# A transformer block on one core with another order of the same operations

## The chip, the cores and the metric

The kernel runs on one core of a Trainium2 chip. A core has five engines that work side by side, each with a queue of its own that it takes strictly in order: TensorE (PE, matmuls), VectorE (DVE), ScalarE (ACT, which evaluates functions), GpSimd (POOL) and SyncE (SP, which here only issues transfers); sixteen DMA engines move the data. Semaphores tie the queues together. Data lie in an on-chip memory of 128 partitions, and PE writes into eight accumulator banks (PSUM), which the other engines read. The metric is the device time of one execution in microseconds, less is better; the median of three executions before is 439.99 us (439.59 to 440.89).

## The reference, cut to what matters

```python
def _A_ref(x, wq, wk, wv, wo, beta):          # x: 1 x 2048 x 576, bf16
    H, Dh, N, L = 32, 18, 4, 512              # 32 heads of 18, 4 segments of 512 tokens
    q, k, v = ...                             # x @ wq, x @ wk, x @ wv, split in heads and segments
    phi = lambda t: jnp.where(t > 0, t + 1.0, jnp.exp(t))
    g = _sigmoid(beta).reshape(1, H, 1, 1)
    M, z = 0, 0
    for s in range(N):
        p = _softmax(qs @ ks^T * Dh ** (-0.5) + causal_mask)
        a_dot = p @ vs
        pq = phi(qs)
        a_mem = (pq @ M) / (pq @ z + 1e-06)
        outs.append(g * a_mem + (1.0 - g) * a_dot)
        pk = phi(ks)
        M = M + pk^T @ vs
        z = z + sum over tokens of pk
    return concat(outs) @ wo

h  = x + _A_ref(_layernorm(x), ...)
h2 = h + gelu(_layernorm(h) @ w1 + b1) @ w2 + b2     # w1: 576 x 4608, w2: 4608 x 576
```

## The kernel before

**Stages.** The 2048 tokens are handled as four segments of four tiles of 128 rows. Per segment s the program has these stages, whose letters stand in the names of its operations: X (first layer normalization: statistics at L814, the centring or scaling at L844 to L848, then a transposition of the result, on PE at L865 for some tiles, by a transfer at L726 for the others), P (the projections to q, k and v, L924, L954 and L971), A (attention: scores at L1151 or L1311, exponential at L1100 or L1102, causal mask at L1163 or L1166 in segment 0 and L1323 or L1325 later, product with the values at L1182 or L1336, read-out of the memory at L1282, then transposition, reciprocal of the row sum and product at L1196 to L1205), M (the update of the memory: product at L1066, sum into `MZacc` at L1076), B (the product with wo, the residual, second layer normalization), C (first feed-forward product, L1466 and L1509, and gelu) and D (second feed-forward product, L1563, and the last sum, L1576). The stages of different segments run beside one another: while ACT is in the exponentials of one segment, PE has projections and feed-forward products of others.

**Some forms that occur below.** One exponential reads four banks in one instruction of 128x2048 (L1100), or two instructions of 128x1024 (L1102) read two banks each. A projection pair is either ten matmuls over all 128 rows (L954), or two halves of matmuls over 64 rows each (L924), between which another engine passes a mark (L930). A copy (`copy`, L733 to L739) moves a bank to memory on ACT or DVE. After segment 0, q and k go through a buffer in DRAM: a copy writes the pad `qk_pad` (L735 or L739), a transfer of SP stores it to `qkd` (L1025), and a transposing transfer brings it back as `qk`.

**What sets the order.** Every operation is added to a graph under a name: the stage's tag and its own, so `M0macc` are the two sums into `MZacc` of segment 0 and `A01mask` the masks of the second unit of segment 0's attention. The table `TIMETABLE` (L27) gives each of them, in the order of their adding, an engine and a rank: the letter is the engine (p PE, a ACT, d DVE, g POOL, s SP; w stands for an exponential or copy that is merged with its partner in one instruction, u for a part of gelu that ACT does straight from the bank), the number the rank. `Graph.add` reads them:

```python
op.start, op.eng = self.timetable[key, n]
```

`Graph.schedule` sorts all operations by rank, hands out banks and buffers in that order (`Buf.pick` takes the one that came free first), and fuses the halves of a projection where nothing of PE stands between them; the program is then emitted in this order, so that the ranks are the order in every engine's queue. There is no other scheduler behind it.

**Names that the change and the prediction touch.** `ones` (L1608, ACT) fills the column of ones beside the values; the ACT memsets (L713) clear the pads `fk_pad` for phi(k); `gate` (L800) is a copy of one element behind which loads are held until the first x has landed; `gates` (L1617 to L1622) compute sigmoid(beta); X00copy and X1apply are copies of the transposed x of tile 0 and the scaling of segment 1's x; P1qkst are the four stores of segment 1's q and k (L1025), P1copy the copies into their pads.

Of the kernel before, what the change touches and what calls it, by code (L numbers as in the profile page):

```python
# [27 lines left out]
    "A00exp": "a84 w85 a114 a131",  # L28
    "A00mask": "g140 g93 d94 g89 g204 d170 g197 g201",
    "A00st0": "p 73 110",  # L30
    "A01comb": "g 208 209 224 225",
    "A01exp": "a148 a155 a162 a165 a174 w186 a168 a169",
    "A01mask": "g153 d156 g164 g163 d193 d190 d189 g207",
    "A01oT": "d 210 250 253 239 242",
    "A01rec": "d 188 206 215 218",
    "A01st0": "p 139 151 173 167",
    "A01swap": "g241 d238",
    "A01val": "p 171 211",
    "A01valT": "d 177 175 212 214",
    "A02comb": "g 360 401",  # L40
    "A02exp": "a198 w199 a281 w283 a226 w227 a232 w247 a290 w291 a306 a312 a326 a328",
    "A02mask": "g 321 268 270 317 244 260 343 351",
    "A02rec": "d 347 365",
    "A02st0": "p 194 256 213 231 286 301 320",
    "A02val": "p 303 322 349 355",
    "A02valT": "d 339 358",
    "A03comb": "g 487 516",
    "A03exp": "a356 a359 a377 a378 a369 a370 a389 a396 a409 w410 a419 w422 a440 w441",
    "A03mask": "d400 g380 d379 g412 g405 g406 g448 g442",
    "A03oT": "d 512 534 510 539 530",  # L50
    "A03rec": "d 431 478",
    "A03st0": "p 354 371 361 388 407 418 423",
    "A03swap": "g 524 529",
    "A03val": "p 413 416 463 472",
    "A03valT": "d 420 476",
    "A1comb": "g685 g711 g739 g754 g809 g819 d866 d874",
    "A1comb2": "d695 g720 g740 g778 g826 g820 d881 d875",
    "A1eg": "a 397 386 482 653 699 748 807 765",
    "A1exp": "a475 w484 a511 w519 a493 a502 a582 w597 a527 w540 a600 a605 a625 w632 a639 w640 a656 w657 a678 a693 a704 w706 a749 a750 "
        "a728 w729 a779 w780 a783 w784 a759 a760 a814 a815 a831 a832 a837 a846 a794 w796",  # L60
    "A1flip": "s 395 374 457 557 572 592 719 659",
    "A1mask": "g494 g532 g586 g587 g591 d609 g541 d613 g681 d675 g680 d663 d665 g736 g735 d715 d744 g751 g772 d752 g764 g793 g785 d801 "
        "g828 g850 g853 g848 d845 d847 g857 g806",
    "A1mem": "p 583 469 683 742 725 795 839 851",
    "A1memT": "d 584 470 696 743 726 808 840 852",
    "A1memfin": "d674 g652 d717 g777 g812 g816 d869 g873",
    "A1oT": "d 769 871 829 899 905",
    "A1pq": "d 499 446 621 727 700 787 825 803",
    "A1rec": "d 644 619 713 745 775 810 868 862",
    "A1rec2": "d 616 684 705 753 786 818 860 872",  # L70
    "A1rg": "g 498 432 620 598 667 781 800 746",
    "A1st": "p 474 503 492 581 523 599 618 638 655 677 703 747 722 766 782 758 811 830 836 791",
    "A1swap": "d877 g904",
    "A1val": "p 588 614 682 737 773 802 855 858",
    "A1valT": "d 589 617 698 738 774 817 856 859",
    "A2comb": "g972 d1014 d1083 g1103 g1174 g1192 d1240 d1222",
    "A2comb2": "d1017 d1055 d1109 g1138 g1175 d1193 g1248 g1226",
    "A2eg": "a 870 854 1015 994 1070 1089 1156 1182",
    "A2exp": "a895 a896 a864 a879 a888 a900 a883 a884 a903 a906 a998 w999 a1020 w1021 a980 w983 a1026 w1027 a1003 w1004 a1091 a1092 "
        "a1048 w1051 a1105 a1115 a1072 w1073 a1114 a1123 a1131 w1132 a1136 a1137 a1179 a1189 a1154 w1155 a1167 w1176",  # L80
    "A2flip": "s 797 844 912 909 1036 933 1053 1066",
    "A2mask": "g918 d962 g880 d916 d955 g913 d930 d952 d1010 g1037 d1034 g1007 g991 d1046 d1012 g1045 g1098 g1088 g1067 d1116 d1140 "
        "d1104 g1145 d1124 g1162 g1196 d1190 g1206 g1200 d1201 g1215 g1213",
    "A2mem": "p 988 1009 1049 1063 1128 1143 1204 1209",
    "A2memT": "d 1006 1032 1059 1081 1129 1144 1205 1210",
    "A2memfin": "g1016 d1042 g1079 g1125 g1172 g1160 d1243 g1223",
    "A2oT": "d 1056 1230 1263 1257 1252",
    "A2pq": "d 940 927 1018 1062 1094 1097 1178 1183",
    "A2rec": "d 1008 1041 1078 1084 1165 1159 1212 1211",
    "A2rec2": "d 971 989 1082 1102 1150 1149 1233 1221",  # L90
    "A2rg": "g 805 911 986 1030 1044 1096 1130 1164",
    "A2st": "p 892 843 887 882 902 993 1019 973 1025 1002 1076 1043 1100 1061 1110 1120 1135 1177 1153 1161",
    "A2swap": "d 1251 1228",
    "A2val": "p 969 966 1038 1086 1122 1147 1207 1216",
    "A2valT": "d 970 968 1080 1087 1127 1148 1208 1217",
    "A3comb": "g1388 g1389 g1473 d1488 d1529 d1527 d1599 d1604",
    "A3comb2": "g1390 d1435 g1496 d1489 d1531 d1572 d1606 d1605",
    "A3eg": "a 1214 1334 1299 1423 1471 1440 1555 1545",
# [1639 lines left out]
```

## Time and profile before

| | |
|---|---|
| median of three executions | 439.99 us (439.59 to 440.89) |
| profiled execution | 440.23 us |
| its span in the trace | 438.5 us |
| PE busy | 430.4 us, 98% of the span |
| ACT, DVE, POOL busy | 298.1, 271.9, 177.4 us |
| granted TensorE clock | 0.999 |
| moved by DMA | 70.09 MB, 160 GB/s |

The span runs from the first to the last instruction of the trace; 1.7 us of the profiled execution's own time lie outside it. The page's view in 40 slices of 11 us each shows the course: the tenths in which each engine is busy.

```profile
PE   8988999999999999999999999999999999999997
PEld 5765677776677676654445766644457775446775
DVE  6898899898888986975785776856535110000110
ACT  6997889998988898767998867688473002565000
POOL 6687757546768416544413468430112020010010
```

PE is full except in the first four slices and the last. DVE and ACT are nearly full until about slice 16, and have much time left from slice 28 on, when only feed-forward products remain. "idle before" in a row of the trace is the time for which the engine stood still ahead of the instruction, and the arrow behind it names what released it. In rows of the timeline the first number is the start, the second the length from the first to the last of the instructions that a row puts together.

### The profile page before, as it was taken

The page shows a single profiled execution, that of the slowest core. Times are in us where ns is not written, and L with a number is a line of the kernel's source. Part 1 is how long each engine was busy: PE and PEld are TensorE (multiplying, and loading weights), DVE is VectorE, ACT ScalarE, POOL GpSimd, SP SyncE. Part 2 cuts the span into 40 slices and gives each one's busy share as a digit, 9 for nine tenths or more (in the row PEclk, how much of TensorE's full clock was granted, in tenths as well). Part 3 has the DMA queues.
Part 4 walks back from the last instruction along what each step waited for, and adds up shares of the span by engine and source line. Part 5 has one row for each costly group of instructions (what it writes and reads, how often), then busy time and mean ns, then how long its engine had stood idle before and what let it go on. Part 6 is the DMA issues. An engine that isn't in the chain of part 4 may idle for free.

```text
span 438.5 us, 12035 instructions
## 1 busy us (share of the span) xinstructions
PE 430.4 (98%) x5053; PEld 275.3 (63%) x5053; DVE 271.9 (62%) x580; ACT 298.1 (68%) x313; POOL 177.4 (40%) x333
## 2 busy tenths in 40 slices
PE   8988999999999999999999999999999999999997
PEld 5765677776677676654445766644457775446775
DVE  6898899898888986975785776856535110000110
ACT  6997889998988898767998867688473002565000
POOL 6687757546768416544413468430112020010010
PEclk9999999999999999999999999999999999999999
DMA  7799699988999866482833574415554431630020
GB/s 230 181 231 225 258 200 258 297 178 241 239 246 327 160 176 184 109 176 83 229 108 76 122 192 147 105 55 176 175 168 126 112 110 55 230 95 1 19 64 28
DMA packets 77126, 70.09 MB, mean 160 GB/s; under 512 B 58000, under 2 KB 64528, under 8 KB 77072
## 3 DMA queue, kind: packets, MB, share of 16 engines
q1 hardware_dynamic: 76928, 69.23, 59.8%
q8 instruction: 39, 0.64, 0.7%
q14 instruction: 15, 0.12, 0.1%
q10 hardware_dynamic: 144, 0.09, 0.1%
HBM read 42.30 MB, written 13.37 MB: 127 GB/s over the span
## 4 chain that ended last, share of the span: by engine, by line
PE 91%; DMA 3%; DVE 2%; SPq 1%; ACT 1%; issue 0%; POOL 0%; ACTq 0%; DVEq 0%
PE bank L1563 33%; PE bank L1466 24%; PE bank L1509 8%; PE bank L924 7%; PE bank L954 7%; PE bank L1311 5%; PE bank L1336 3%; DMA x<-in_A_x_dram 2%; DMA qkd<-qk_pad 2%; PE bank L1151 1%; PE bank L1285 1%; PE bank L1282 1%; SPq L719 1%; PE bank L1182 1%; PE bank L1066 1%; SPq L726 0%
## 5 line engine op out<-in xcount | busy, mean ns | idle before, releaser
L1563 PEld LDWEIGHTS <-hT 128*128 128x128 bf16 x1152 | 110.4, 98 | 33.8 <-issue 6.1
L1466 PE MATMUL bank<-xreg,w1g 64*128 64x512 bf16 x972 | 108.2, 376 | 0.0
L1100 ACT ACTIVATE pt<-bank 128x2048 bf16<-128x2048 f32 x41 | 77.0, 1877 | 19.6 <-PE bank L1311 10.4
L1102 ACT ACTIVATE pt<-bank 128x1024 bf16<-128x1024 f32 x78 | 75.7, 1022 | 17.4 <-PE bank L1311 11.3
L1466 PEld LDWEIGHTS <-w1g 64*128 64x128 bf16 x972 | 46.8, 94 | 55.7 <-issue 2.8
L1563 PE MATMUL bank<-w,hT 128*128 128x288 bf16 x576 | 77.3, 286 | 0.0
L1563 PE MATMUL bank<-w_lo,hT 128*128 128x288 bf16 x576 | 76.9, 286 | 0.0
L1576 DVE TENSOR_TENSOR ot<-bank,hc 128x288 bf16<-128x288 f32 x32 | 14.2, 454 | 89.0 <-PE bank L1563 82.4
L1472 ACT ACTIVATE hT<-bank,b_col 128x512 bf16<-128x512 f32 x36 | 22.4, 688 | 47.8 <-PE bank L1466 47.7
L1325 POOL TENSOR_SCALAR_AFFINE_SELECT pt<-pt 128x512 bf16<-128x512 bf16 x60 | 39.4, 669 | 32.4 <-ACT pt L1100 19.3
L1549 POOL TENSOR_TENSOR hc<-hc,b_bc 128x576 f32<-128x576 f32 x13 | 16.7, 1287 | 80.7 <-DMA hc<-hd 80.7
L1432 ACT ACTIVATE hT<-hT 128x3072 bf16<-128x3072 bf16 (+8 forms) x18 | 39.8, 2260 | 0.1
L1509 PE MATMUL bank<-xreg,w1g 64*128 64x256 bf16 x648 | 38.1, 269 | 0.1
L1509 PEld LDWEIGHTS <-w1g 64*128 64x128 bf16 x648 | 30.6, 94 | 6.4 <-issue 2.9
L954 PE MATMUL bank<-hT,xreg 128*128 128x288 bf16 x252 | 34.5, 287 | 0.0
L1482 ACT ACTIVATE hT<-bank,b_col 128x512 bf16<-128x512 f32 x36 | 22.9, 684 | 11.3 <-PE bank L1466 11.0
L954 PEld LDWEIGHTS <-xreg 128*128 128x128 bf16 x252 | 23.1, 98 | 8.0 <-issue 0.9
L924 PE MATMUL bank<-hT,xreg 64*128 64x288 bf16 x292 | 23.8, 285 | 0.5 <-ACT pt L1102 0.5
L1311 PE MATMUL bank<-qk 32*128 32x512 bf16 (+3 forms) x384 | 23.8, 301 | 0.0
L1297 POOL TENSOR_TENSOR t<-t,r 128x288 f32<-128x288 f32 x13 | 9.3, 717 | 34.7 <-DVE r L1294 34.6
L1291 DVE STREAM_TRANSPOSE t<-bank 128x512 f32<-128x512 f32 x24 | 16.7, 701 | 7.6 <-PE bank L1282 4.4
L1344 DVE STREAM_TRANSPOSE t<-bank 128x512 f32<-128x512 f32 x24 | 16.4, 692 | 6.7 <-PE bank L1336 5.9
(128 smaller groups left out, 580.3 us busy)
## 6 DMA issues: line engine op xcount, KB each, us to landing
w1g<-in_B_w_dram SPq DMA_DIRECT2D x41, 576.0 KB, 4.4
qkd<-qk_pad SPq DMA_DIRECT2D x12, 512.0 KB, 4.6
hd<-h SPq DMA_DIRECT2D x16, 288.0 KB, 3.9
hc<-hd SPq DMA_DIRECT2D x16, 288.0 KB, 3.7
w_lo<-in_B_w_dram SPq DMA_DIRECT2D x3, 864.0 KB, 6.7
w<-in_B_w_dram SPq DMA_DIRECT2D x3, 864.0 KB, 9.2
xb<-in_A_x_dram SPq DMA_DIRECT2D x16, 144.0 KB, 4.2
out_dram<-ot SPq DMA_DIRECT2D x15, 144.0 KB, 3.6
```

The lines of the kernel that those rows point to most:

```text
L924: return nc.tensor.matmul(out=half(hf), lhsT=xTb.t[r, k, ts], rhs=wt[r, hf, k, :], start=start, stop=stop, skip_group_check=True)
L954: nc.tensor.matmul(out=half(hf), lhsT=xTb.t[:, k, ts], rhs=wt[:, hf, k, :], start=(k == 0 and b.form != "first"), stop=(k == n - 1 and b.f ...
L1100: nc.scalar.activation(out=pt.t[:], in_=banks_all[:, st[0].n:st[0].n + 4, :], func=ACT.Exp, scale=scale)
L1102: nc.scalar.activation(out=pt.t[:, 2 * j:2 * j + 2, :], in_=st[j].t[:], func=ACT.Exp, scale=scale)
L1311: nc.tensor.matmul(out=st[i // 2].t[:, i % 2, off:off + n_], lhsT=qk[rows, 1, kt * P:(kt + 1) * P], rhs=qk[rows, 0, kt * P:L], start=True, ...
L1325: nc.gpsimd.affine_select(out=blk, in_=blk, pattern=[[0, 4], [1, P]], compare_op=ALU.is_ge, fill=0.0, base=0, channel_multiplier=-1)
L1432: nc.scalar.activation(out=at, in_=at, func=ACT.Gelu_apprx_tanh)
L1466: nc.tensor.matmul(out=cc[w].t[:], lhsT=w1.t[rows, k, q, :], rhs=x2T[s].t[rows, k, :], start=(k == 0), stop=(k == ND - 1))
L1472: ready_f[f + w] = [add(pf - 12, {"act": 0.68}, lambda e, f=f, w=w, cc=cc: nc.scalar.activation(out=hT[:, :, f + w, :], in_=cc[w].t[:].rea ...
L1482: nc.scalar.activation(out=dst, in_=src, func=ACT.Identity if e == "act" else ACT.Gelu_apprx_tanh, bias=b)
L1509: nc.tensor.matmul(out=cc[w].t[:, q * 2 * P:(q + 1) * 2 * P], lhsT=w1.t[rows, k, q, :], rhs=x2T[s].t[rows, k, ts], start=(k == 0), stop=(k ...
L1563: nc.tensor.matmul(out=c.t[:, 0:c1 - c0], lhsT=hT[:, tl // 2, f, (tl % 2) * P:(tl % 2 + 1) * P], rhs=w2_c[ch][:, f - ch * WCH, c0:c1], sta ...
```

## The change

The program has the same 1904 operations with the same names, before and after. Only the numbers and letters of `TIMETABLE` differ, in nearly all of its 320 lines; `Graph` and all stages are the same text. A few of the lines, those of which the prediction speaks:

```diff
-    "A00exp": "a84 w85 a114 a131",
+    "A00exp": "a 74 78 103 111",
-    "A01mask": "g153 d156 g164 g163 d193 d190 d189 g207",
+    "A01mask": "g163 d156 g158 g162 d188 d198 g207 d194",
-    "A01rec": "d 188 206 215 218",
+    "A01rec": "d 186 202 223 217",
-    "M0macc": "d 203 196",
+    "M0macc": "d 205 203",
-    "P1qkst": "s 282 254 336 332",
+    "P1qkst": "s 290 213 332 307",
-    "X00copy": "a 22 29 31 36",
+    "X00copy": "a25 d33 a31 a35",
-    "X1apply": "d 185 172",
+    "X1apply": "d 214 173",
-    "P1copy": "d233 a237 a338 d166 a192 a228 d314 a323 a297 a259 a292 d382",
+    "P1copy": "d232 a241 a344 d177 a189 a233 d313 a327 a297 a253 a293 d385",
-    "P01copy": "a118 d137 a105 a102 a107 a138",
+    "P01copy": "d123 d137 d93 a87 a98 a138",
-    "C00copy": "d368 w372 d362 w363 d403 w404 d443 w447 d414 w415 d481 d485 d490 w491 d496 w501 d504 w505",
+    "C00copy": "d376 w377 d364 w367 d403 a420 d434 w455 d424 w431 d489 w490 d461 w469 d495 d496 d511 w512",
...
-    "gate": "g 13",
+    "gate": "d 9",
-    "gates": "a95 d96",
+    "gates": "a95 d169",
-    "memset": "d24 g32 g5 d11 a45 a54 a112 a113 g426 g53 g6",
+    "memset": "d8 g7 g36 d65 a26 a94 a58 a109 g427 g14 g328",
-    "ones": "a 417 47",
+    "ones": "a 38 16",
```

As the letters say, the change moves operations between engines as well: over the program 12 merged exponentials become halves, 33 parts of gelu instead of 21 are done straight from the bank, and PE has 16 more matmuls, since two projection pairs that were fused now have other work between their halves.

Three places show what it moves. The first is ACT's queue at the start of the program. Here x_64 holds the first x, xn_142 and xn_143 its centred copies, mean_b their row sums, and xreg is the transposed x that the projections read. Before:

```order
L825 ACTIVATE xn_142,mean_b_108<-x_64 128x288
L825 ACTIVATE xn_143,mean_b_109<-x_64 128x288
L846 ACTIVATE xn_142<-x_64,mean_b_108 128x2x128
L735 COPY xreg<-bank 128x3x128
L846 ACTIVATE xn_143<-x_64,mean_b_109 128x2x128
L735 COPY xreg<-bank 128x2x128
L735 COPY xreg<-bank 128x3x128
L735 COPY xreg<-bank 128x2x128
L713 ACTIVATE fk_pad_138<-fk_pad_138 128x32x7
L1608 ACTIVATE v_aug_116<-ident 128x128
```

Now:

```order
L825 ACTIVATE xn_142,mean_b_108<-x_64 128x288
L1608 ACTIVATE v_aug_116<-ident 128x128
L825 ACTIVATE xn_143,mean_b_109<-x_64 128x288
L846 ACTIVATE xn_142<-x_64,mean_b_108 128x2x128
L735 COPY xreg<-bank 128x3x128
L713 ACTIVATE fk_pad_138<-fk_pad_138 128x32x7
L846 ACTIVATE xn_143<-x_64,mean_b_109 128x2x128
L735 COPY xreg<-bank 128x3x128
L735 COPY xreg<-bank 128x2x128
L1608 ACTIVATE v_aug_115<-ident 128x128
```

The first of the two `ones` (L1608, v_aug_116) has moved from behind the copies to between the two halves of the mean, the clearing of fk_pad_138 to ahead of the second centred copy, and one of the copies of 128x2x128 is gone from ACT; it stands on DVE now, ahead of its first statistics.

The second is DVE's queue where unit A01 of segment 0's attention ends (its masks are the L1163 x3, its transposed outputs t, its reciprocals r), and where the first memory is copied into MZacc. Before:

```order
L1163 TENSOR_TENSOR pt_72<-pt_72,tri 128x2x256
L848 TENSOR_SCALAR xn_142<-x_65,ln_102 128x640
L1196 STREAM_TRANSPOSE t_89<-bank 128x512
L1196 STREAM_TRANSPOSE t_90<-bank 128x512
L848 TENSOR_SCALAR xn_143<-x_65,ln_103 128x640
L1200 RECIPROCAL r_110<-t_90 128x16
L1201 TENSOR_TENSOR r_110<-r_110,omg_q 128x16
L1163 TENSOR_TENSOR pt_71<-pt_71,tri 128x2x256 x3
L1076 COPY MZacc<-bank 128x304 x2
L1200 RECIPROCAL r_111<-t_89 128x16
L1201 TENSOR_TENSOR r_111<-r_111,omg_q 128x16
L1221 STREAM_TRANSPOSE oT_69<-o_nat_95 128x256
```

Now:

```order
L848 TENSOR_SCALAR xn_142<-x_65,ln_101 128x640
L739 CAST qk_pad_136<-bank 128x8x4x18
L1042 SCALAR_TENSOR_TENSOR fk_pad_141<-ek_87,rk_88 128x32x18
L1196 STREAM_TRANSPOSE t_89<-bank 128x512
L1200 RECIPROCAL r_110<-t_89 128x16
L1201 TENSOR_TENSOR r_110<-r_110,omg_q 128x16
L1196 STREAM_TRANSPOSE t_90<-bank 128x512
L1163 TENSOR_TENSOR pt_71<-pt_71,tri 128x2x256 x3
L1200 RECIPROCAL r_111<-t_90 128x16
L1201 TENSOR_TENSOR r_111<-r_111,omg_q 128x16
L1076 COPY MZacc<-bank 128x304 x2
L1221 STREAM_TRANSPOSE oT_69<-o_nat_95 128x256
```

The scaling of x into xn_143 (L848) has left the place ahead of the masks and stands behind them. One reciprocal with its product (L1200, L1201) stands ahead of the two copies into MZacc instead of behind them. The scaling into xn_142, a cast into a pad and a product for phi(k) (L1042) stand just ahead of the transpositions, and the three operations of `gates` (L1620 to L1622) ahead of these, where before they stood some fifteen rows earlier.

The third is SP's queue at the same time. qkd_148 is the buffer in DRAM for segment 1's q and k, x and xb are loads of x for the normalization and for the residual, ot_81 and b_bc the biases, w1g weights of the first feed-forward product. Before:

```order
L726 DMA_TRANSPOSE w_lo<-qk_pad_136 128x8x128
L719 DMA ot_81<-in_B_b_dram 128x36
L719 DMA b_bc<-in_B_b_dram 128x576
L719 DMA x_64<-in_A_x_dram 128x2x640
L719 DMA xb_66<-in_A_x_dram 128x576
L1025 DMA qkd_148<-qk_pad_137 128x2048
L719 DMA xb_67<-in_A_x_dram 128x576
L719 DMA x_65<-in_A_x_dram 128x2x640
L726 DMA_TRANSPOSE xreg<-xn_143 128x5x128
L1025 DMA qkd_148<-qk_pad_136 128x2048
```

Now:

```order
L726 DMA_TRANSPOSE w_lo<-qk_pad_137 128x8x128 x2
L719 DMA x_64<-in_A_x_dram 128x2x640
L719 DMA b_bc<-in_B_b_dram 128x576
L726 DMA_TRANSPOSE xreg<-xn_142 128x5x128
L1025 DMA qkd_148<-qk_pad_136 128x2048
L719 DMA xb_66<-in_A_x_dram 128x576
L719 DMA w1g_97<-in_B_w_dram 128x2304
L719 DMA ot_81<-in_B_b_dram 128x36
L719 DMA x_65<-in_A_x_dram 128x2x640
L719 DMA xb_67<-in_A_x_dram 128x576
L726 DMA_TRANSPOSE xreg<-xn_143 128x5x128
L1025 DMA qkd_148<-qk_pad_137 128x2048
```

The first store of q and k (L1025) stood behind the loads of both biases, of x_64 and of xb_66; now it stands ahead of xb_66, of one of the biases and of the weights w1g_97, which before had been issued earlier. The loads of x_65 and xb_67 remain between it and the second store, with w1g_97 and ot_81 now beside them.

606 rows, old and new, of the table TIMETABLE are left out of this document.

## The prediction

> **What bounds the kernel now.** I read the page's busy times first, then TensorE's waits, then busy time by stretch, then the end of the chain of waits, and last the rows of the first 45 us.
>
> ```profile
> span 438.5 us, 12035 instructions
> PE 430.4 (98%) x5053; PEld 275.3 (63%) x5053; DVE 271.9 (62%) x580; ACT 298.1 (68%) x313; POOL 177.4 (40%) x333
> ```
>
> TensorE (PE) is busy for 430.4 of 438.5 us. An order that only moves work of the other engines can therefore win at most what PE idles, 438.5 - 430.4 = 8.1 us, less the start and the tail, which no order removes. The view of PE's waits says where it idles:
>
> ```profile
> PE bank L1182 <- DVE pt L1163: 1.1, 1, 1.1
> PE bank L748 <- PEq L1722: 0.8, 1, 0.8
> PE bank L954 <- ACT qk_pad L735: 0.6, 1, 0.6
> PE bank L924 <- ACT pt L1102: 0.5, 1, 0.5
> PE bank L865 <- DVE xn L844: 0.5, 1, 0.5
> PE bank L1151 <- ACT pt L1100: 0.4, 1, 0.4
> PE bank L865 <- DVE xn L848: 0.3, 1, 0.3
> PE bank L971 <- DMA hT<-in_A_w_dram: 0.3, 1, 0.3
> PE bank L1151 <- DVE qk_pad L739: 0.2, 1, 0.2
> ```
>
> Nine waits, 4.7 us together. Busy time by stretch shows where they lie (PE is the number behind the length):
>
> ```profile
> 0.00:12.00 12.00, 10.41 (x72) 6.40 (x73) 7.61 (x24) 7.86 (x17) 7.74 (x22) 1.00 0.78 244
> 12.00:28.00 16.00, 15.57 (x287) 10.93 (x284) 14.75 (x34) 14.89 (x21) 11.76 (x30) 1.00 0.86 174
> 28.00:46.00 18.00, 15.22 (x243) 10.29 (x232) 16.66 (x41) 15.21 (x14) 14.05 (x29) 1.00 0.97 260
> 46.00:90.00 44.00, 43.88 (x756) 32.33 (x755) 39.24 (x79) 40.08 (x39) 26.63 (x64) 1.00 0.91 247
> 90.00:210.00 120.00, 120.00 (x1566) 77.45 (x1562) 98.77 (x207) 101.69 (x97) 66.44 (x115) 1.00 0.78 191
> 210.00:330.00 120.00, 120.00 (x1263) 66.50 (x1260) 81.30 (x169) 92.69 (x90) 42.16 (x67) 1.00 0.51 142
> ```
>
> From 46 to 330 us PE loses 44.00 - 43.88 = 0.12 us in all: the body has nothing to win, only something to lose. All that can be won stands before 46 us, and most of it between 28 and 46 us, where VectorE (DVE) is busy for 16.66 of 18.00 us. The end is one block of matmuls behind another:
>
> ```profile
> 329.55 35.28 PE bank L1563 x288
> 364.83 35.07 PE bank L1466 x324
> 399.90 35.40 PE bank L1563 x288
> ```
>
> **The change part by part.** It changes only the table of ranks and engines, so the sum is over four parts: PE's own work, the first 45 us, the body, the end.
>
> *PE's own work.* Two projection pairs that ran as 10 full-row matmuls (L954) now run as 18 half-row ones (L924): 16 more matmuls. The chain of waits has the step of the half-row form:
>
> ```profile
> 315.32 0.61 PE bank L924 x10
> ```
>
> Ten take 0.61 us, so 18 take 1.10. The full-row form is shown by 8 matmuls of L954 that take 1.15 us with one change of row mode in them (40.69 below): ten take 1.2 to 1.4. That is between -0.3 and 0 us a pair; but a pair that turns full into half rows can cost a change of row mode on either side, and over the whole program such changes go from 225 to 223. I take -0.2 us for all of it (bounds -0.6 and +0.2).
>
> *The first 12 us.* ScalarE (ACT) now writes the column of ones (L1608) between its two halves of the mean, and zeroes a pad (L713) ahead of its second centred copy; one copy of transposed x goes from ACT to DVE.
>
> ```profile
> 3.63 0.44 ACT L825 ACTIVATE xn<-x 128x288 bf16<-128x288 bf16 x1
> 4.14 0.51 ACT L846 ACTIVATE xn<-x,mean_b 128x256 bf16<-128x256 bf16 x1
> ...
> 6.14 1.27 PE L971 MATMUL bank<-hT,xreg 128*128 128x288 bf16 x9
> ...
> 6.75 0.40 ACT L713 ACTIVATE fk_pad<-fk_pad 128x224 uint32<-128x224 uint32 x1
> 7.05 0.76 ACT L1608 ACTIVATE v_aug<-ident 128x128 bf16<-128x128 bf16 x1
> ```
>
> The ones (0.76) push the second half of the mean from 3.63 to 4.39 and the centred copy from 4.14 to 4.90; the zeroing adds 0.40, and the copy that left ACT gives some 0.2 back. Laid end to end, the first projection (L971) starts about 0.95 us later than 6.14. Part of that meets waits that stand there anyway: 0.3 for the weights (L971 <- DMA) and 0.3 for xn L848. About 0.35 us of it is left behind them, and from here on DVE's queue decides.
>
> *DVE from 12 to 36 us.* DVE has 14.75 of 16.00 us busy and no reserve here. Counting its rows up to the first transposition of attention outputs (L1196), it gains one copy of 128x2x128 (0.4, an estimate by the 0.44 that ACT takes over 128x288 at 3.63), the gate (0.1) and two casts (0.75 each, row 27.55), and loses one scaled cast and one copy of 128x8x128, which I take for a cast each: 0.4 + 0.1 + 1.5 - 1.5 = +0.5 us. These rows carry it, with those on which PE then waits:
>
> ```profile
> 27.55 0.75 DVE L739 CAST qk_pad<-bank 128x576 bf16<-128x576 f32 x1
> 28.22 0.41 DVE L1163 TENSOR_TENSOR pt<-pt,tri 128x512 bf16<-128x512 bf16 x1
> ...
> 31.15 2.45 DVE L1163 TENSOR_TENSOR pt<-pt,tri 128x512 bf16<-128x512 bf16 x3
> 33.53 0.84 DVE L1076 COPY MZacc<-bank 128x304 f32<-128x304 f32 x2
> 33.66 0.74 PE L1182 MATMUL bank<-pt,v_aug 128*19 128x128 bf16 x40 [1.12 <-DVE pt L1163]
> 34.29 0.24 DVE L1200 RECIPROCAL r<-t 128x16 f32<-128x16 f32 x1
> 34.57 0.17 DVE L1201 TENSOR_TENSOR r<-r,omg_q 128x16 f32<-128x16 f32 x1
> ```
>
> The last of the three masks (L1163) released PE at 33.66. With +0.5 us of DVE work ahead, and the 0.1 to 0.5 us by which the rows between shift, I get PE 0.6 to 1.0 us late there. Behind the masks the change puts the reciprocal and its product (0.24 + 0.17, with their gaps 0.45) ahead of the two copies into MZacc (L1076), which stood before them: the banks that these copies free come 1.05 to 1.45 us late. Middle: +1.25.
>
> *DMA queue of SP at 33 to 44 us.* The third and fourth wait of 28 to 46 us hang on a store of q and k and on what comes back from it:
>
> ```profile
> 34.56 0.38 SPq L1025 DMA_DIRECT2D qkd<-qk_pad  x1
> 40.69 1.15 PE L954 MATMUL bank<-wt_o,oT 128*128 128x288 bf16 x8
> 41.71 0.64 ACT L735 CAST qk_pad<-bank 128x576 bf16<-128x576 f32 x1 [1.30 <-POOL ln L829]
> 42.40 1.14 PE L954 MATMUL bank<-wt_o,oT 128*128 128x288 bf16 x8 [0.56 <-ACT qk_pad L735]
> ```
>
> The cast at 41.71 writes the pad that the store of 34.56 reads, so it cannot start before that store has landed; PE waited 0.56 for it and, right behind, 0.41 for an exponential (L1100) that ACT does after the cast. The change issues this store ahead of xb_66 and of a bias that stood before it, and of the weights w1g_97, which had gone out earlier. Two issues of 0.4 to 0.5 us (this row has 0.38) less stand ahead of it, so it should go out about a microsecond sooner, and PE comes 1.25 us late, so both waits, 0.97 us, should be gone. Net of the first 46 us: 1.25 - 0.97 = +0.3. Lower bound: if the three masks run at the 0.41 of the one at 28.22, not the 0.82 that each took here, 1.25 - 3 x 0.41 - 0.97 = -0.9. Upper bound: nothing is given back, +1.45.
>
> Each of the masks on DVE ran beside selects on GpSimd (POOL). The Trainium skill (SBUF — State Buffer, "Who interferes with whom") says that a VectorE tensor_tensor with both inputs in SBUF and a GpSimd operation that reads SBUF exclude one another for the whole instruction. The 0.41 against 0.82 of these rows points the same way. By that rule each mask could be held for a whole select of 0.67 (the page's group of L1325), giving three times 0.41 + 0.67 - 0.82 = 0.26, 0.8 us more than my sum.
>
> *The body, 46 to 330 us.* ACT gives 12 of its merged exponentials (L1100) back to two halves (L1102), and evicts fewer banks of the first feed-forward product by copy and more by gelu straight from the bank. By the page 41 merged ones at 1877 ns stand against halves of 1022: a split costs 2 x 1022 - 1877 = 167 ns of ACT, twelve 2.0 us, and it starts its second half with the first two banks already released. ACT has 120 - 102 = 18 us free from 90 to 210 us, so this is hidden; if it were not, 2.0 us.
>
> ```profile
> L1100 ACT ACTIVATE pt<-bank 128x2048 bf16<-128x2048 f32 x41 | 77.0, 1877 | 19.6 <-PE bank L1311 10.4
> L1102 ACT ACTIVATE pt<-bank 128x1024 bf16<-128x1024 f32 x78 | 75.7, 1022 | 17.4 <-PE bank L1311 11.3
> L1325 POOL TENSOR_SCALAR_AFFINE_SELECT pt<-pt 128x512 bf16<-128x512 bf16 x60 | 39.4, 669 | 32.4 <-ACT pt L1100 19.3
> ```
>
> What can be lost is a bank that comes back late. Laying these durations out in the new order I find three places: the first feed-forward product of segment 0 (L1509, near 70 us) behind an eviction that stands after six other DVE rows, 0.3 to 0.4 us; the scores near 115 us behind a merged exponential, 0.1 to 0.2; and L1466 near 308 us, 0.1. Some of this is met by the shifts before it. I take +0.3 (bounds -0.1, all that PE idles here, and +1.1, three times 0.37).
>
> *The end* is the same 288, 324 and 288 matmuls and the same add and store: 0.
>
> **Sum.** The profiled execution took 440.23 us, of which the span is 438.5 and 1.7 lie around it. 440.23 - 0.2 + 0.3 + 0.3 + 0 = 440.6. The median of the three runs, 439.99, stands 0.24 below the profiled time, so I forecast **440.4 us** for the median. The bounds add up to 440.4 + (-0.6 + 0.2) + (-0.9 - 0.3) + (-0.1 - 0.3) = 438.4 and 440.4 + 0.4 + 1.15 + 0.8 = 442.75.
>
> **Rivals.**
>
> *Faster: the head's waits vanish.* The waits of 28 to 46 us are 0.16 + 0.52 + 1.12 + 0.56 + 0.41 = 2.77 us. If PE comes late to each by the 0.35 us of the first 12 us and DVE's masks do not move, they are absorbed: 439.99 - 2.77 + 0.35 = 437.6. For it: all hang on an operation off PE. Against it: DVE is busy 16.66 of 18 there, and PE's lateness comes from DVE's own rows. Chance 0.27.
>
> *Slower: DVE's queue of 12 to 36 us sets the end.* One mechanism: at the masks and MZacc copies DVE comes late by its whole upper bound, 1.45, the 0.97 stays because the store lands when the other transfers leave room (DMA share 0.97 from 28 to 46 us), and the body loses its 0.3: 439.99 - 0.2 + 1.45 + 0.3 = 441.5, and with the masks held by whole selects 442.3. It decides once the last mask of unit A01 ends more than 1.2 us later than 33.6. For it: no DVE reserve. Against it: the earlier store. Chance 0.22.
>
> *Slower: the body pays.* After 46 us PE makes good nothing, since it never idles; every late bank stays in the time. Four waits of the head's size, 0.4, in 284 us give 440.4 - 0.3 + 1.6 = 441.7. For it: 98% busy, with each wait covered narrowly. Against it: ACT and POOL get less work than before. Chance 0.13.
>
> *No change, my forecast:* 0.38, its own range 438.9 to 441.3.
>
> **How the numbers follow.** A measurement of this kernel tells about 0.3% from no change, 1.3 us, so the borders are 438.7 and 441.3. Faster is the first rival, 0.27; slower the other two, 0.22 + 0.13 = 0.35; the forecast 0.38. The range runs from the faster rival's 437.6 over the slower ones' 442.3 to the sum's upper bound: 437.6 to 442.8.
>
> **What would show it.** Right: PE's list of waits has again some nine entries, that on DVE L1163 about as long or longer, those on ACT L735 and L1100 near 44 us gone; the first L971 starts near 7.1 us; the first block of 288 L1563 at the end starts at 329.4 to 330.5, and the 105.8 us from there to the last matmul stand as before. Wrong: the last A01 mask ends before 33 us (first rival), or PE loses over 1 us between 46 and 330 us (third).

## The result, and the profile after

The changed kernel takes 442.13 us (median of six executions, 441.66 to 442.48) against 440.22 for the kernel before in the same session (439.59 to 441.06): ratio 1.0041, 95% interval 1.0027 to 1.0055. It is slower by a little more than the 0.3% that the prediction drew as its border, and lies inside its range of 437.6 to 442.8; the likeliest case, no change at 440.4, did not come, its "slower" did. The profiled execution took 441.80 us with a span of 439.9, 1.4 us more than before. In one of the experiments (headAfk_bodyB) one execution of twelve, the profiled one, was disturbed (869.79 us) and is left out.

The page of the changed kernel, spans and busy times:

```profile
span 439.9 us, 12070 instructions
PE 431.1 (98%) x5069; PEld 275.5 (63%) x5069; DVE 279.7 (64%) x578; ACT 294.7 (67%) x314; POOL 173.2 (39%) x331
```

DVE is busy for 7.8 us more, with two instructions fewer. Part is plain work (the view by lines has five more of the sums of L1549 on DVE than before, 0.8 us each, which POOL lost). Part is the same work taking longer, and that is where this case turns. TensorE's waits in the changed kernel (us in total, times, longest):

```profile
PE bank L1151 <- DVE h L1393: 1.2, 1, 1.2
PE bank L1151 <- DVE qk_pad L739: 0.9, 1, 0.9
PE bank L748 <- PEq L1722: 0.8, 1, 0.8
PE bank L1509 <- DVE hT L1523: 0.6, 2, 0.4
PE bank L924 <- DVE qk_pad L739: 0.5, 1, 0.5
PE bank L865 <- DVE xn L844: 0.3, 1, 0.3
PE bank L1509 <- DMA w1g<-in_B_w_dram: 0.2, 1, 0.2
PE bank L1151 <- DVE MZacc L1076: 0.2, 1, 0.2
PE bank L1151 <- ACT pt L1100: 0.2, 1, 0.2
PE bank L1336 <- DVE t L1291: 0.2, 1, 0.2
```

Of the large waits of before only the one at the very start (L748, 0.8) is left: 1.1 for the mask L1163, 0.6 for L735 and 0.5 for L1102 are gone. New ones of the same size stand in their place, and nearly all of them name DVE. Busy time by stretch (PE is the number behind the length):

```profile
12.00:28.00 16.00, 15.42 (x286) 11.12 (x283) 15.28 (x34) 15.40 (x23) 11.16 (x29) 1.00 0.95 188
28.00:46.00 18.00, 15.37 (x240) 10.24 (x227) 17.52 (x38) 15.54 (x16) 12.79 (x27) 1.00 0.97 266
46.00:90.00 44.00, 43.23 (x762) 32.30 (x761) 40.54 (x84) 39.89 (x41) 30.12 (x73) 1.00 0.89 212
90.00:210.00 120.00, 119.64 (x1555) 77.17 (x1551) 100.25 (x197) 100.01 (x90) 66.81 (x110) 1.00 0.79 197
```

From 46 to 210 us PE now idles 0.77 + 0.36 = 1.13 us, where it idled 0.12. From 12 to 46 us it idles 0.58 + 2.63 = 3.21 us, exactly as long as before (0.43 + 2.78). A mark that both kernels share shows how even the head is: up to the 16 matmuls of L954 near 60 us PE's queue holds the same matmuls in both, with a few in another order. These 16, before and after:

```profile
59.91 2.13 PE L954 MATMUL bank<-hT,xreg 128*128 128x288 bf16 x16
59.93 2.13 PE L954 MATMUL bank<-hT,xreg 128*128 128x288 bf16 x16
```

They start 0.02 us apart. This is one execution of each kernel, though, and the mark scatters: three versions below whose order of the head is the same (a_fk_early, headAfk_bodyB_2, afk_to143_B) have it at 59.60, 58.76 and 58.91 us, and are as far apart at 24 us already. So the mark says that the heads are even to within about 0.8 us, and no more. The three blocks at the end (the chain of waits of the changed kernel):

```profile
330.88 35.39 PE bank L1563 x288
366.26 35.07 PE bank L1466 x324
401.33 35.40 PE bank L1563 x288
```

330.88 - 329.55 = 1.33 us late, and from there to the last sum as before. So of the span's 1.4 us the head carries nothing in these two executions and the stretch from 60 to 330 us, the body, 1.3. The length of the body does not hang on the start: from the mark to the first block it is 269.64 us before and 269.65 to 269.80 in the three versions below that have the body of before (best_gates, headAfk_bodyB_2, s_headA_bodyB), 270.95 in the change, and 270.39 to 270.79 in the three that have its body (a_fk_early, a_fk_late, a_fk_gates).

### The profile page after: what moved, and what is told of

Same layout as the page of the kernel before. It is cut to its first block, busy times and chain, and to the rows that moved or that the text cites. A ratio compares the mean times of both kernels' runs of the same rounds, so it can differ in the third digit from the quotient of the medians.

```text
span 439.9 us, 12070 instructions
## 1 busy us (share of the span) xinstructions
PE 431.1 (98%) x5069; PEld 275.5 (63%) x5069; DVE 279.7 (64%) x578; ACT 294.7 (67%) x314; POOL 173.2 (39%) x331
## 4 chain that ended last, share of the span: by engine, by line
PE 88%; DVE 7%; DMA 2%; issue 1%; ACT 1%; SPq 0%; DVEq 0%; ACTq 0%
PE bank L1563 31%; PE bank L1466 24%; PE bank L1509 7%; PE bank L924 7%; PE bank L954 5%; PE bank L1311 4%; PE bank L1336 3%; PE bank L971 1%; DMA w1g<-in_B_w_dram 1%; DVE ln L814 1%; PE bank L748 1%; DVE fk_pad L1042 1%; DMA ot<-in_B_b_dram 1%; PE bank L1285 1%; PE bank L1151 1%
## 5 line engine op out<-in xcount | busy, mean ns | idle before, releaser
L1563 PEld LDWEIGHTS <-hT 128*128 128x128 bf16 x1152 | 110.3, 98 | 34.1 <-issue 6.7
L1466 PE MATMUL bank<-xreg,w1g 64*128 64x512 bf16 x972 | 107.8, 376 | 0.0
L1102 ACT ACTIVATE pt<-bank 128x1024 bf16<-128x1024 f32 x88 | 85.2, 1022 | 24.2 <-PE bank L1311 14.9
L1466 PEld LDWEIGHTS <-w1g 64*128 64x128 bf16 x972 | 46.2, 94 | 56.7 <-issue 3.0
L1100 ACT ACTIVATE pt<-bank 128x2048 bf16<-128x2048 f32 x36 | 67.6, 1877 | 17.6 <-PE bank L1311 10.2
L1563 PE MATMUL bank<-w_lo,hT 128*128 128x288 bf16 x576 | 77.2, 286 | 0.0
L1563 PE MATMUL bank<-w,hT 128*128 128x288 bf16 x576 | 76.9, 286 | 0.1
L1325 POOL TENSOR_SCALAR_AFFINE_SELECT pt<-pt 128x512 bf16<-128x512 bf16 x63 | 43.5, 699 | 48.5 <-ACT pt L1102 27.1
L1472 ACT ACTIVATE hT<-bank,b_col 128x512 bf16<-128x512 f32 x36 | 22.3, 688 | 48.0 <-PE bank L1466 47.6
L1509 PE MATMUL bank<-xreg,w1g 64*128 64x256 bf16 x648 | 38.5, 269 | 0.8 <-DVE hT L1523 0.6
L1432 ACT ACTIVATE hT<-hT 128x4096 bf16<-128x4096 bf16 (+6 forms) x12 | 34.0, 2866 | 2.6 <-DVE hT L1488 2.5
L1509 PEld LDWEIGHTS <-w1g 64*128 64x128 bf16 x648 | 31.1, 94 | 7.0 <-issue 3.2
L1482 ACT ACTIVATE hT<-bank,b_col 128x512 bf16<-128x512 f32 x40 | 25.3, 693 | 10.6 <-PE bank L1466 10.2
L954 PE MATMUL bank<-hT,xreg 128*128 128x288 bf16 x228 | 31.4, 287 | 0.0
L924 PE MATMUL bank<-hT,xreg 64*128 64x288 bf16 x340 | 26.2, 284 | 0.5 <-DVE qk_pad L739 0.5
L954 PEld LDWEIGHTS <-xreg 128*128 128x128 bf16 x228 | 20.9, 98 | 7.5 <-issue 1.2
L1311 PE MATMUL bank<-qk 32*128 32x512 bf16 (+3 forms) x384 | 23.8, 301 | 0.1
L924 PEld LDWEIGHTS <-xreg 64*128 64x128 bf16 x340 | 16.2, 94 | 9.2 <-issue 5.5
L830 POOL TENSOR_TENSOR ln<-ln,mhalf 128x1 f32<-128x1 f32 x32 | 18.6, 580 | 2.7
```

Of the source, the lines that this page charges most:

```text
L924: return nc.tensor.matmul(out=half(hf), lhsT=xTb.t[r, k, ts], rhs=wt[r, hf, k, :], start=start, stop=stop, skip_group_check=True)
L954: nc.tensor.matmul(out=half(hf), lhsT=xTb.t[:, k, ts], rhs=wt[:, hf, k, :], start=(k == 0 and b.form != "first"), stop=(k == n - 1 and b.f ...
L1100: nc.scalar.activation(out=pt.t[:], in_=banks_all[:, st[0].n:st[0].n + 4, :], func=ACT.Exp, scale=scale)
L1102: nc.scalar.activation(out=pt.t[:, 2 * j:2 * j + 2, :], in_=st[j].t[:], func=ACT.Exp, scale=scale)
L1311: nc.tensor.matmul(out=st[i // 2].t[:, i % 2, off:off + n_], lhsT=qk[rows, 1, kt * P:(kt + 1) * P], rhs=qk[rows, 0, kt * P:L], start=True, ...
L1325: nc.gpsimd.affine_select(out=blk, in_=blk, pattern=[[0, 4], [1, P]], compare_op=ALU.is_ge, fill=0.0, base=0, channel_multiplier=-1)
```

## The experiments

Each kernel is an edit of the table alone. The times beside a ratio are medians of the same session, and the kernel before was timed with each group: 440.26, 440.51 and 440.44 us in the three groups.

**What is 1.18 us at 42.84 us?** The timeline of the changed kernel around the longest new wait:

```profile
39.32 2.41 POOL L1166 TENSOR_SCALAR_AFFINE_SELECT pt<-pt 128x512 bf16<-128x512 bf16 x4
39.91 2.43 DVE L1042 SCALAR_TENSOR_TENSOR fk_pad<-ek,rk 128x576 bf16<-128x576 bf16 x1
42.26 0.81 DVE L814 BATCH_NORM_STATS2 ln<-x 128x6 f32<-128x288 bf16 x2
43.23 0.74 DVE L1393 TENSOR_TENSOR h<-bank,xb 128x576 f32<-128x576 f32 x1
44.02 0.40 PE L1151 MATMUL bank<-w_lo,qk 32*128 32x256 bf16 x8 [1.18 <-DVE h L1393]
```

PE waits for the residual sum L1393, which frees a bank; that sum stands in DVE's queue behind a product for phi(k), L1042. The median of its twelve executions is 0.75 us; this one takes 2.43, beside four selects of POOL one behind another, and three others take 0.95 to 1.17. In the kernel before all twelve took 0.71 to 0.76 us. *a_fk_early* moves it by four rows on DVE, so that it runs ahead of the selects; no other engine's order changes:

```diff
-    "P1fk": "d 301 259 419 358",
+    "P1fk": "d 301 236 419 358",
```

> The changed kernel with one row of VectorE moved: the product for phi(k) of P1fk.1 (L1042), which took 2.43 us instead of 0.75 beside four selects of GpSimd in a row at 39.91 us, goes ahead of them, by four rows. Theory 'held by the selects': the row takes 0.75 us again, the residual sum L1393 comes about 1.7 us sooner, TensorE's wait of 1.18 us at 42.84 falls to under 0.3, and the span is 0.9 to 1.2 us shorter than 439.9. Rival 'VectorE's queue is full whatever its order': the same work stands ahead of L1393, the wait and the span change by less than 0.3 us.

440.75 us, ratio 1.0011 (1.0002 to 1.0021), 1.4 us under the change. The row is quick again, the residual sum starts at 42.89, and this wait is no longer in PE's list:

```profile
39.64 0.76 DVE L1042 SCALAR_TENSOR_TENSOR fk_pad<-ek,rk 128x576 bf16<-128x576 bf16 x1
40.88 2.41 POOL L1166 TENSOR_SCALAR_AFFINE_SELECT pt<-pt 128x512 bf16<-128x512 bf16 x4
42.89 0.76 DVE L1393 TENSOR_TENSOR h<-bank,xb 128x576 f32<-128x576 f32 x1
```

The times of day are 1.2 us later in this execution. About half of that is PE's longer waits for its first weights (0.40) and for L739 (0.75 instead of 0.49); the order of the rows is what counts. The rival, a queue that is full in any order, falls: the same work stands ahead of L1393.

*a_fk_late* moves the same row the other way, behind two statistics and their aggregate, still beside the selects:

```diff
-    "P1fk": "d 301 259 419 358",
+    "P1fk": "d 301 262 419 358",
```

> The same row moved the other way, behind the two statistics (0.81 us) and their aggregate (0.21) that follow it, so that it starts about 1.0 us later but still beside the selects, which end near 41.7 us. Theory 'held by the selects': it ends near 42.4 us as before, whatever its start, and so takes about 1.4 us instead of 2.43; L1393 starts 0.6 to 0.8 us sooner and TensorE's wait of 1.18 us falls by as much. Rival 'this row is slow in itself here' (its operands, its place in memory): it takes 2.4 us again and the wait stays at 1.1 to 1.3 us.

440.91 us, ratio 1.0015 (1.0006 to 1.0023). Its timeline:

```profile
39.27 2.41 POOL L1166 TENSOR_SCALAR_AFFINE_SELECT pt<-pt 128x512 bf16<-128x512 bf16 x4
40.80 1.49 DVE L1042 SCALAR_TENSOR_TENSOR fk_pad<-ek,rk 128x576 bf16<-128x576 bf16 x1
42.22 0.74 DVE L1393 TENSOR_TENSOR h<-bank,xb 128x576 f32<-128x576 f32 x1
43.01 0.40 PE L1151 MATMUL bank<-w_lo,qk 32*128 32x256 bf16 x8 [0.22 <-DVE h L1393]
```

The row started 0.89 us later and ended at 42.29, where it had ended at 42.34. Its end is set by the end of the selects (41.68, and 41.73 in the change), 0.61 us behind it both times, and not by its start. So it is held by the selects. Moving it later was as good as moving it earlier, because the statistics that now run in its place are not held (the two take 0.78 us beside the selects, and took 0.81 behind them).

*a_selects_late* leaves the row where it is and moves the selects, by putting two small operations of POOL that wait for DVE ahead of them:

```diff
-    "B00rstd": "g 285",
+    "B00rstd": "g 273.5",
```

> The change with its phi(k) row left where it is; GpSimd's two small operations for a layer normalization (L829, L830), which wait for statistics behind the residual sum L1393, stand ahead of the four selects instead of behind them, so the selects start only after 43 us. Theory 'held by the selects': L1042 takes 0.75 us at 39.9 us, L1393 starts near 41.6 instead of 43.23, TensorE's wait of 1.18 at 42.84 falls under 0.3 (other waits may grow behind the later selects), time 0.2 to 0.3% under the change's 442.13. Rival 'the row is slow at this place whatever GpSimd does': 2.4 us again, wait and time as the change.

The row takes 0.72 us at its old place, with the same rows of DVE around it:

```profile
40.47 0.72 DVE L1042 SCALAR_TENSOR_TENSOR fk_pad<-ek,rk 128x576 bf16<-128x576 bf16 x1
45.13 2.63 POOL L1166 TENSOR_SCALAR_AFFINE_SELECT pt<-pt 128x512 bf16<-128x512 bf16 x4
```

The time was missed, though: 445.84 us, ratio 1.0124 (1.0108 to 1.0139). What is queued on POOL behind the late selects is late too, and PE's list has these two instead of the wait of 1.18:

```profile
PE bank L1151 <- DVE qk_pad L739: 2.9, 2, 2.0
PE bank L865 <- DVE xn L848: 1.7, 1, 1.7
```

Part of the loss is the clock. These two waits end at 52.13 and 54.61 us, and from 55 to 58 us TensorE's granted clock is 0.50 of full speed, where it is 1.00 in the change; the mean over the run is 0.996 in all four executions.

**Head or body?** *s_headB_bodyA* takes the first 360 ranks from before and the rest in the order of the change; *s_headA_bodyB* does the reverse. In the traces the queues first differ from the order they began with at about 57 us on DVE (later than the 50 expected), 53 on SP and 70 on PE. All later ranks are numbered anew in the order of the second table, so each diff is long; against the changed kernel, two of its lines each:

```diff
-    "P1fk": "d 301 259 419 358",
-    "gates": "a95 d169",
+    "P1fk": "d 307 217 423 369",
+    "gates": "a95 d96",
```

```diff
-    "A1val": "p 587 621 687 739 774 796 851 861",
-    "C1gelu": "a 1237 1316 1332",
+    "A1val": "p 588 614 682 737 773 802 855 858",
+    "C1gelu": "a 1239 1301 1333",
```

> The order of before for the first 360 ranks (to about 50 us on VectorE), then the order of the change. Theory 'the body costs, the head is even': TensorE's waits of the head are those of before (about 4.9 us with the start), those near 65 to 72 us and at 131 to 187 us are those of the change (about 1.1 us), and the time is 0.8 to 1.5 us over before. Rival 'the head costs': within 0.4 us of before.

444.27 us, ratio 1.0085 (1.0068 to 1.0102), more than either theory allowed. The seam has a wait of its own, 2.1 us at 59.1 (L924 <- DVE hT L1523), since DVE's rows of the one table stand behind rows of the other that wait for POOL. It was read in the quickest of the six executions (442.39 us); the three slowest, at 444.62 to 444.69 us, have a mean granted clock of 0.995 to 0.996, the other three 1.0. So what the seam costs cannot be taken off the median, and this run decides nothing.

> The order of the change for the first 360 ranks, then the order of before. Theory 'the body costs, the head is even': TensorE's wait of 1.18 us at 42.84 is there, no wait over 0.15 us after 60 us, and the time is within 0.4 us of before. Rival 'the head costs': 1 us or more over before.

441.12 us, ratio 1.0021 (1.0007 to 1.0034), span 439.0. Its mark near 60 us stands at 59.94, the wait of 1.18 is there, and behind 60 us PE has no wait over 0.12. The time lies between the two theories. With the body of before the change loses 0.9 us (0.3 to 1.5 by the interval), with its own body 1.9 (1.2 to 2.4). Nearly half of the loss shows with the head alone in these times, though the mark of the profiled execution is even with before; with these intervals and the scatter of the mark, the head's share is rough.

**Does DVE's queue from 12 to 36 us set the head?** *a_fk_gates* starts from a_fk_early and moves the three operations of the gates (L1620 to L1622) behind the cast for which PE waits 0.89 us at 28.17; two operations of POOL that read the gates follow them:

```diff
-    "gates": "a95 d169",
-    "gmz": "g 273 267 446 170",
+    "gates": "a95 d177.5",
+    "gmz": "g 273 267 446 178.2",
...
-    "omg": "g 174",
+    "omg": "g 178.4",
```

> The change with the phi(k) row moved ahead of the selects, and the three operations of the gates (L1620 to L1622, 1.0 us at 26.86) moved from ahead of the scaling L848 and the cast L739 to behind them. Theory of the prediction 'VectorE's queue has no reserve from 12 to 36 us': TensorE's wait of 0.89 at 28.17 for the cast falls to under 0.2, but the same work still stands ahead of the last mask, so the wait there (L1182, 0.14) grows by 0.4 to 0.9 and the time stays within 0.4 us of a_fk_early (440.75). Rival 'only the place of the cast counts': the wait goes and nothing takes its place, 0.7 to 0.9 us less.

441.22 us, ratio 1.0029 (1.0008 to 1.0049), 0.5 us over a_fk_early, with intervals that overlap. The wait for the cast is gone and came back at the masks, where it had stood in the kernel before. Its timeline:

```profile
31.10 1.23 POOL L1166 TENSOR_SCALAR_AFFINE_SELECT pt<-pt 128x512 bf16<-128x512 bf16 x2
31.79 2.40 DVE L1163 TENSOR_TENSOR pt<-pt,tri 128x512 bf16<-128x512 bf16 x3
33.10 0.82 POOL L1166 TENSOR_SCALAR_AFFINE_SELECT pt<-pt 128x512 bf16<-128x512 bf16 x1
34.25 0.73 PE L1182 MATMUL bank<-pt,v_aug 128*19 128x128 bf16 x38 [1.19 <-DVE pt L1163]
```

In the changed kernel the same three masks took 1.54 us, with one select beside them:

```profile
31.48 1.54 DVE L1163 TENSOR_TENSOR pt<-pt,tri 128x512 bf16<-128x512 bf16 x3
31.59 0.82 POOL L1166 TENSOR_SCALAR_AFFINE_SELECT pt<-pt 128x512 bf16<-128x512 bf16 x1
33.31 0.85 DVE L1076 COPY MZacc<-bank 128x304 f32<-128x304 f32 x2
```

One of them took 0.85 us, beside the select, the other two 0.44 and 0.41. In the kernel before POOL had these rows there:

```profile
29.85 2.67 POOL L1166 TENSOR_SCALAR_AFFINE_SELECT pt<-pt 128x512 bf16<-128x512 bf16 x4
32.49 0.83 POOL L1205 TENSOR_TENSOR o_nat<-t,r 128x288 bf16<-128x288 f32 x1
```

The last two of these four selects (from 31.11 us on) and the product ran beside the masks, which began at 31.15. So the three masks take 2.45 us beside two selects and a product in the kernel before, 2.40 beside two selects and a product here (31.70 to 33.92 us), and 1.54 beside one select in the change. What POOL does at that moment sets the masks' length more than the order of DVE's own rows.

**Where in the body?** *afk_to104_B* and *afk_to143_B* take a_fk_early for the first 620 and 845 ranks (to about 104 and 143 us on PE), then the order of before. Against a_fk_early, one line each:

```diff
-    "A1val": "p 587 621 687 739 774 796 851 861",
+    "A1val": "p 587 621 683 737 773 802 855 858",
```

```diff
-    "A1val": "p 587 621 687 739 774 796 851 861",
+    "A1val": "p 587 621 687 739 774 796 858 860",
```

> The change with the phi(k) row moved for the first 620 ranks (to about 104 us on TensorE), then the order of before. Theory 'the body costs between 120 and 230 us': as headAfk_bodyB, at most 0.5 us above it. Rival 'the waits of 65 to 72 us cost': 0.6 us or more above headAfk_bodyB, as a_fk_early.

445.33 us, ratio 1.0111 (1.0085 to 1.0136): the seam itself makes a wait of 3.76 us at 110.4 (L924 <- ACT qk_pad L735), and from 116 to 119 us the granted clock is 0.50. It answers nothing.

> The same for the first 845 ranks (to about 143 us on TensorE), then before. Theory 'several waits of 0.1 to 0.15 us at 130, 143, 172 and 186 us, with the restart of TensorE behind each, make the body's loss': between afk_to104_B and a_fk_early, about 0.2 to 0.6 us above the first. Rival 'one place in 104 to 143 us makes all of it': as a_fk_early.

441.82 us, ratio 1.0029 (1.0015 to 1.0043), over a_fk_early and not under it, with a wait of 0.60 us at 201 (L1311 <- DVE hT L1488) that neither parent has. So the body could not be cut in pieces in this way. What remains are the waits in the change's own trace: 0.19 for weights at 65.2, 0.18 and 0.40 for evictions (L1523) at 68.7 and 72.8, and three of 0.10 to 0.15 at 131.0, 143.8 and 187.3. The largest:

```profile
71.56 1.21 DVE L1523 TENSOR_TENSOR hT<-bank,b_col 128x1024 bf16<-128x1024 f32 x1
72.82 1.38 PE L1509 MATMUL bank<-xreg,w1g 64*128 64x256 bf16 x22 [0.40 <-DVE hT L1523]
```

They add up to 1.14 us against 0.12 before. Of the 1.3 us of the body 0.3 is left. Part of that may be how a wait is counted, from the modelled end of the matmul ahead of it: from start to start the step across the wait of 0.10 at 131.0 takes 0.37 us, where the same pair of lines (L1509, then L1311) takes 0.20 without a wait, and the step across the one of 0.11 at 187.3 takes 0.40, where L1563 behind L1563 takes 0.12. The other four were not taken apart in this way.

**A version that beats both.** *headAfk_bodyB* is a_fk_early for the first 360 ranks, then the order of before; *headAfk_bodyB_2* is the same kernel once more. Against a_fk_early:

```diff
-    "A1val": "p 587 621 687 739 774 796 851 861",
-    "C1gelu": "a 1237 1316 1332",
+    "A1val": "p 588 614 682 737 773 802 855 858",
+    "C1gelu": "a 1239 1301 1333",
```

> The first 360 ranks of the change with the phi(k) row moved ahead of the selects, then the order of before. Theory 'the head of the change is the better one once that row is free, the body of before the better body': about 0.9 us under before at 60 us, kept to the end, so 439.2 to 439.7, 0.1 to 0.25% under before. Rival 'what the head wins is lost again at later waits': within 0.3 us of before, with a new wait of TensorE between 60 and 330 us.

440.04 us, ratio 0.9991 (0.9977 to 1.0005): not to be told from before in this group.

> The same kernel as headAfk_bodyB, whose profiled execution was disturbed, for a profile that can be read and more times: 0.9 us under before at 60 us, no wait of TensorE over 0.2 us after 60 us, 0.05 to 0.25% under before in time.

439.68 us, ratio 0.9985 (0.9975 to 0.9994), span 437.7. Behind rank 360 only the body differs from a_fk_early (440.75 us, 1.0002 to 1.0021), and these two intervals do not meet (that of the first group, up to 1.0005, just does): in times, too, the body of the change costs about 1 us. The mark, at 58.76, stands 1.15 us earlier than before (59.91), a little more than its scatter, and the only wait of PE behind it is one of 0.12 at 67.1.

*best_gates* moves the gates in it the other way than a_fk_gates did, to where DVE stood idle (they start at 17.17 us), and their exponential on ACT (L1617) with them:

```diff
-    "gates": "a95 d169",
+    "gates": "a87 d93",
```

> headAfk_bodyB with the gates' three operations moved from 26.9 us on VectorE to 16.6 us, into the 0.31 us for which VectorE stands idle there, away from the selects beside which they took 1.0 instead of 0.7 us. Theory 'VectorE's queue from 12 to 36 us sets the head': 0.4 to 0.7 us less VectorE work ahead of the masks, and as much off the waits of 28 to 35 us, unless masks meet more selects; 0.1 to 0.15% under headAfk_bodyB. Rival 'the selects beside them set the masks' length': the masks take 2.4 us instead of 1.5 and it is no faster.

439.24 us, ratio 0.9977 (0.9968 to 0.9986): faster than both kernels, 0.23% under before. Between it and headAfk_bodyB_2 the intervals overlap, and of the two profiled executions that of headAfk_bodyB_2 has the shorter span (437.7 against 437.9 us), so a gain in time by the place of the gates is not shown; the waits alone show it. Its waits from 28 to 35 us sum to 0.52 + 0.13 + 0.17 = 0.82 us, against 0.89 + 0.16 + 0.14 + 0.17 = 1.36 in headAfk_bodyB_2, and the masks kept their short form:

```profile
32.11 1.53 DVE L1163 TENSOR_TENSOR pt<-pt,tri 128x512 bf16<-128x512 bf16 x3
32.15 0.88 POOL L1166 TENSOR_SCALAR_AFFINE_SELECT pt<-pt 128x512 bf16<-128x512 bf16 x1
```

## Why the prediction was right and wrong

**The frame held.** The body had nothing to win, the head's waits were traded against one another, and the end was the same: 105.88 us from the first block of L1563 to the last sum (436.76 - 330.88) against 105.78.

**PE's own work, -0.2 us.** From start to start, all matmuls of L954 and L924 together take 0.41 us less than before (2.05 less in L954's 16 fewer, 1.64 more in L924's 32 more), inside the bounds. The forms were misread: a fused pair is eight matmuls of L954 and two of L924, not ten of L954, so two pairs move 16 and 32. PE's busy time rose by 0.7 us all the same; where is open.

**The first 12 us: 0.95 us late at the first L971.** Mis-sized. It started at 6.50, 0.36 later than before:

```profile
3.66 0.74 ACT L1608 ACTIVATE v_aug<-ident 128x128 bf16<-128x128 bf16 x1
3.92 0.71 ACT L825 ACTIVATE xn<-x 128x288 bf16<-128x288 bf16 x1
4.63 0.49 ACT L846 ACTIVATE xn<-x,mean_b 128x256 bf16<-128x256 bf16 x1
```

The sum laid the ones and the second half of the mean end to end; the rows overlap by half a microsecond (3.66 + 0.74 = 4.40, and L825 begins at 3.92), so that the centred copy came at 4.63 and not at 4.90. By 14 us nothing of the 0.36 was left: two waits of before, 0.26 for weights and 0.31 for xn L848, were gone.

**DVE at 28 to 36 us: masks 0.6 to 1.0 late, MZacc 1.05 to 1.45 late.** This step failed. The masks ended at 33.02, 0.6 us earlier than before (33.61), and the copies into MZacc started at 33.31 against 33.53. The working took the masks' 0.82 us of before as their price; their price is 0.4 alone, and 0.8 beside a select or a product of POOL. Nor did each mask of before run beside a select, as the prediction says: two did, and the third ran beside the product L1205. In the change two selects are over ahead of the masks, at 29.14 to 30.77 us, and only one stands beside them. The prediction had this as its lower bound (masks at 0.41) and did not follow it: the selects' own places in POOL's queue were not laid beside DVE's.

**The store of q and k: both waits near 44 us gone.** Right: neither L735 nor L1100 near 44 us stands in the list after. (They are the fourth and fifth wait from 28 us on, not the third and fourth.)

**The net of the head, +0.3 us.** The mark says +0.02, to within its scatter, and the times of s_headA_bodyB say 0.9 (0.3 to 1.5): the sum's 0.3 is inside, but not by its own steps. The wait at the masks fell from 1.12 to 0.14, and those at the store (0.97) went. Two losses met them. For the cast L739 PE now waits 0.89 us at 28.2, where it waited 0.16, and 0.49 at 23.3, where it did not wait. The other loss no step foresaw: four selects of unit A02, which in the kernel before ran one, two and one at 39.95, 42.24 and 44.91 us, now stand together at 39.32 beside L1042 and held it for 2.43 - 0.75 = 1.7 us, 1.18 of which PE waited. That the selects hold this row, and that the row makes this wait, was shown by three runs; a_fk_early, which frees it, takes back 1.4 of the change's 1.9 us. That an overrated loss at the masks and an unseen one at this row nearly cancelled is luck. The slower rival of the head named the right kind of mechanism, masks held by selects, at the wrong place.

**The body, +0.3 us (bounds -0.1 and +1.1).** Mis-sized: 1.3 us, over its upper bound. Of the three places only the first came, L1509 near 70 us with 0.40 (and 0.18 just ahead of it); the scores near 115 and L1466 near 308 did not wait, and a wait for weights at 65 us and three small waits at 131 to 187 us came unannounced. The exponentials were counted wrong as well: the traces have 36 merged ones (L1100) after and 41 before, five fewer on balance and not twelve, which changes nothing, as ACT hid them. The third rival, "the body pays", had the sign and the size (441.7) with six waits in place of its four; the sign that the prediction named for it, over 1 us lost by PE between 46 and 330 us, came with 1.13. Part of them followed from the head: with the phi(k) row freed, PE's idle time from 46 to 90 us fell from 0.77 to 44.00 - 43.72 = 0.28 us, and the wait for weights at 65 us went.

**The chances.** No change was put at 0.38 and slower at 0.35; with the border at 0.3% the measured ratio of 1.0041, whose interval reaches down to 1.0027, lies just on the slower side. The likeliest case was off by 1.7 us, of which 1.0 is the body's term. Of the signs for being right, the number of waits, the two waits gone near 44 us and the length of the end came; a long wait for L1163, a first L971 near 7.1 us and a first block of L1563 by 330.5 us (it stands at 330.88) did not. So the time lies in the range, and the account of the store and of the end held, but the head's masks and the size of the body did not.

## What to carry to other kernels

When a change of order moves GpSimd's work, lay its new places beside VectorE's rows with two inputs in on-chip memory: here such a row was held by a single operation of GpSimd at some places and by a run of four selects at one, and it cost time only where a matmul hung on the next row of VectorE's queue. A price read from a trace holds for the neighbours it was read beside, so for an operation whose length varies in one kernel look first at what the other engine did at that moment. In a kernel whose TensorE is never idle behind some point, every wait of a tenth of a microsecond stays in the time, and the few long waits ahead of that point may change places without changing the sum.

## What the runs showed of the hardware that was not expected

A run of GpSimd selects can hold a VectorE row to its end: two starts 0.89 us apart (39.91 and 40.80), ends 0.05 us apart (42.34 and 42.29), each 0.61 us behind the last of four selects. The Trainium skill (SBUF — State Buffer, "Who interferes with whom") has the exclusion for a whole instruction; here it lasted over the four in a row, not one of 0.6 us, so that the price was 1.7 us where the prediction's reading of the rule gave 0.26 a row. It is not always so. In the changed kernel the same line, earlier, stands beside two selects:

```profile
21.07 1.74 POOL L1166 TENSOR_SCALAR_AFFINE_SELECT pt<-pt 128x512 bf16<-128x512 bf16 x2
21.29 1.02 DVE L1042 SCALAR_TENSOR_TENSOR fk_pad<-ek,rk 128x576 bf16<-128x576 bf16 x1
```

Here the row ends 0.61 us behind the first select (21.71), and it is the second select that takes longer, 1.15 us instead of 0.63. The masks got in between two selects in the same way. Why the row gets in at one place and not at the other is open; no run tried it.

A long wait of TensorE can cost clock as well as time. The granted clock was 0.50 from 116 to 119 us in afk_to104_B, whose wait of 3.76 us ended at 114.19, and from 55 to 58 us in a_selects_late, whose waits of 1.97 and 1.65 us ended at 52.13 and 54.61. In the profiled s_headB_bodyA, with one wait of 2.13 us, it stayed at 1.00. What decides between the two is not shown: two of the twelve executions of a_fk_gates (444.09 and 445.06 us) also have a mean clock of 0.996, and for them there is no profile.

Waits too short for the lists count: PE's idle time from 90 to 210 us, 0.36 us in the table by stretch, is spread over three places of 0.10 to 0.15 us, two of them under the smallest entry of the list.
